# One attention and two-layer feed-forward kernel on one core: a different start-up (centroids, zeros, square root) and a new order of the planned work

## The chip, the cores and the metric

The kernel runs on one core of a Trainium2 chip. The metric is the device time of one execution, in microseconds (us). Three executions of the kernel before took 782.28, 782.38 and 784.30 us; their median, 782.38 us, is the time before.

The names of the engines are those of the profile: PE is TensorE, DVE is VectorE, ACT is ScalarE, POOL is GpSimd, SP is the engine whose queue issues the transfers. PEld is the loading of weights into PE, which overlaps with PE. A line such as L640 is line 640 of the kernel before.

## What is computed

Attention in which a query sees only the keys of its own cluster, for 2 x 8 heads of 768 rows and 64 columns, followed by two feed-forward stages:

```python
q_n, k_n, c_n = (each row divided by its norm + 1e-6)
q_assign = argmax(einsum('bhsd,hcd->bhsc', q_n, c_n), axis=-1)   # 16 clusters a head
k_assign = argmax(einsum('bhsd,hcd->bhsc', k_n, c_n), axis=-1)
scores = where(q_assign == k_assign, q @ k.T / 8, -1e9)
x = (softmax(scores) @ v)            # to 1536 tokens x 512
h = x @ w_in;  y = (h - tanh(h)) @ w_out
out = (sigmoid(y @ w_gate) * (y @ w_val)) @ w_out2
```

The assignment needs the norms of the centroids only (a query's own norm does not change its argmax), so the kernel normalises `centroids` and leaves `q` and `k` as they are.

## The kernel before

**The planner.** Nearly all work is written down as tasks: `add(engine, cost, priority, function, dependencies, buffers)`. The class `Planner` (from L271) then plays them through with the modelled costs and emits the functions in the order that comes out. The priority of task n is `ORDER[n] / 1000`, from a list of numbers that a search made (L39 on); among the tasks of an engine that could start within a window (`AHEAD`, from the parameters `AH_PE` to `AH_SP` at L27) the one with the lowest number goes first. Each engine then works through its own queue strictly in the order emitted, and waits on the chip for what an instruction needs.

**What is not planned.** What is written straight into the function, outside `add`, comes ahead of all planned work of its engine, and the planner's clock knows nothing of it. Before L613 that is: the filler's operand `busy` (L583), the identity matrices (L586 to L588), small constants on POOL (L589 to L601), and the zeros:

```python
for i in range(NS):                                   # L606, NS = 3 buffers "stk"
    if PRM["NAT"]:
        nc.vector.memset(tiles["stk", i].bitcast(F32)[0:96]...., 0.0)   # L608, 96 x 3072
    nc.gpsimd.memset(tiles["stk", i].bitcast(F32)[96:97, 3, :], 1.0)    # L609
```

**The start-up.** `rawq` and `rawk` (the first two heads, 2 x 192 KB each) and `rawv` are loaded by SP (L710, L908). Between the two loads SP issues that of the centroids, `cn` (L625). The centroids are normalised by three planned tasks: `cn_square` on ACT (L628 square with the row sum in `ss`, L629 square root, L630 one exponential that serves to load the table of the exponential again), `cn_scale` on DVE (L633 to L635), and a transpose on PE (L640); `cn_place` on DVE (L645) puts the result into `cb`. Meanwhile PE transposes `rawq` and `rawk` (L721, three at a time, two halves each, in the order q, k, q, k), ACT copies the results out as `xtq`, `xtk` (L725), and for the first two heads ACT and POOL write their high and low parts into `stk` (L737, L741). With `cb`, `xtq` and `xtk` PE makes the 24 scores of the clusters (L772); DVE finds the winners and makes them one-hot (L781 to L792); PE turns them (L863), ACT writes them into `stk` (L867). After that the heads' work proper begins: matmuls L936, L1003 and L1056, exponentials L1006 and L1059, low parts on POOL and DVE L1022 and L1070, products with `v` L1082 to L1084. The feed-forward part follows (L1369, L1732), for which the weights are loaded, cut and split meanwhile.

**The filler.** 110 planned tasks of two small matmuls on zeros (L652, operand `busy`) have the lowest priority of PE; the planner puts one wherever PE could start nothing else, until all 110 are used up. Their number (`N_BUSY`) is the same before and after, and the psum bank that they write is free for other work only after the last of them.

Of the kernel before, what the change touches and what calls it, by code (L numbers as in the profile page):

```python
# [27 lines left out]
    QUEUE=2.4, AH_PE=0.1147, AH_ACT=0.2895, AH_DVE=0.0311, AH_POOL=2.0837, AH_SP=1.2656, N_BUSY=110, NR=2,  # L28
    NRH=1, HX=['hx', 'hhxx'], WAR=0.8, LM=9, LV=9, ZP1=-12.307, ZP=1.419, FD=0.1631, FO=0.8005, LOQ=0, VHI=0,
# [399 lines left out]
def tile_cluster_attention_moe(  # L429
# [41 lines left out]
    def c_acts(n):  # L471
        return 0.10 + 0.00084 * n
# [73 lines left out]
    NS = 3  # L546
# [59 lines left out]
    for i in range(NS):  # L606
        if PRM["NAT"]:
            nc.vector.memset(tiles["stk", i].bitcast(F32)[0:96].rearrange("p a n -> p (a n)"), 0.0)  # L608
        nc.gpsimd.memset(tiles["stk", i].bitcast(F32)[96:97, 3, :], 1.0)  # L609
# [1326 lines left out]
```

## Time and profile before

| | before |
|---|---|
| median of three executions | 782.38 us |
| the profiled execution: its own time | 784.97 us |
| the profiled execution: span from first to last instruction | 782.8 us |
| PE busy | 770.6 us (98% of the span) |
| DVE, ACT, POOL busy | 73%, 58%, 72% |
| share of PE in the chain that ended last | 93% |

The page of a profile gives the busy time of each engine, the chain of work that ended last (followed back from the last instruction to what released it) and the costliest groups of instructions. The trace behind it can be asked for the busy time in chosen stretches, the waits of an engine with what ended them, and the instructions in order of time. A busy PE is not a useful PE: the filler counts as busy, and so does a matmul that runs at half clock.

### The profile page before, as it was taken

Reading aid. Unit: us, or ns where it says so; the run is one execution under the profiler, and the core shown is the slowest. Engines: PE = TensorE matmul, PEld = TensorE weight load, DVE = VectorE, ACT = ScalarE, POOL = GpSimd, SP = SyncE. Lnnn points to the kernel's source line nnn. Section 1 sums busy time; section 2 is a strip of 40 time slices with the busy share of each in tenths; the row PEclk is TensorE's granted clock in tenths of the full one; section 3 lists DMA queues with packets and bytes.
Section 4 is the critical chain, followed back from the end, with each engine's and each line's share of the span. In section 5 each row is a group of like instructions: output and inputs, shape, how many; then the busy total and the mean of one; then the engine's idle time right before and its main releaser. Section 6 shows DMA issues by size and latency. Waiting matters only on the chain.

```text
span 782.8 us, 15756 instructions
## 1 busy us (share of the span) xinstructions
PE 770.6 (98%) x5905; PEld 728.4 (93%) x5905; DVE 573.6 (73%) x1110; ACT 457.5 (58%) x883; POOL 567.1 (72%) x604
## 2 busy tenths in 40 slices
PE   7999999999999999999999999999999999999998
PEld 6988899898889999999999999999998989899997
DVE  6697878887986978877576878976465786765434
ACT  4588888889887644544554455765462635253250
POOL 6249777778979795787797699699593978665261
PEclk8999999999999999999999999999999999999999
DMA  4597755665642100422131323003220332310004
GB/s 103 133 182 157 165 128 137 145 154 133 152 129 81 59 1 0 135 69 68 54 95 41 108 68 107 14 29 107 68 82 27 98 119 69 93 63 20 1 1 161
DMA packets 75571, 69.57 MB, mean 89 GB/s; under 512 B 39252, under 2 KB 60072, under 8 KB 75496
## 3 DMA queue, kind: packets, MB, share of 16 engines
q1 hardware_dynamic: 75496, 68.58, 32.6%
q8 instruction: 46, 0.75, 0.4%
q14 instruction: 29, 0.24, 0.1%
HBM read 45.12 MB, written 3.15 MB: 62 GB/s over the span
## 4 chain that ended last, share of the span: by engine, by line
PE 93%; DVE 5%; ACT 1%; issue 1%; POOL 0%; DVEq 0%; ACTq 0%; POOLq 0%
PE over_left L1369 17%; PE over_left L1732 15%; PE sm L1732 10%; PE sm L1369 10%; PE over_right L1369 8%; PE over_right L1732 6%; PE bb L1056 3%; PE bc L1056 2%; PE ba L1056 2%; PE sm L1082 2%; PE sm L1083 2%; PE sm L1084 2%; PE sm L772 2%; PE ba L936 1%; DVE finr L940 1%; PE bc L936 1%
## 5 line engine op out<-in xcount | busy, mean ns | idle before, releaser
L1070 POOL TENSOR_TENSOR pt<-pf,pt 128x768 f16<-128x768 f32 x46 | 77.3, 1694 | 19.4 <-ACT pt L1059 9.5
L1070 POOL TENSOR_TENSOR ptt<-pf,ptt 128x768 f16<-128x768 f32 x29 | 49.8, 1723 | 13.4 <-ACT pf L1059 8.2
L1732 PE MATMUL over_left<-xh,stk 128*128 128x384 f32 x186 | 54.7, 335 | 0.0
L1369 PE MATMUL over_left<-stk,w 128*128 128x384 f32 x178 | 46.4, 337 | 0.0
L1082 PE MATMUL sm<-vs,pt 128*128 128x65 f16 x318 | 43.4, 194 | 0.2 <-DVE xl L1121 0.2
L1083 PE MATMUL sm<-vs,pt 128*128 128x64 f16 x318 | 43.2, 195 | 0.0
L1084 PE MATMUL sm<-vs,pt 128*128 128x65 f16 x318 | 42.9, 192 | 0.0
L1748 ACT ACTIVATE pf<-over_left 128x384 f32<-128x384 f32 x40 | 19.6, 489 | 33.0 <-PE over_left L1732 31.7
L940 DVE TENSOR_REDUCE finr<-ba 128x1 fp32r<-128x768 f32 x35 | 33.2, 948 | 5.6 <-PE ba L936 2.7
L1400 ACT ACTIVATE stk<-pf 128x384 fp32r<-128x384 f32 x43 | 22.3, 523 | 25.0 <-POOL pf L1803 6.9
L1402 POOL TENSOR_TENSOR oht<-pf,stk 128x384 fp32r<-128x384 f32 x23 | 23.4, 1018 | 16.5 <-ACT stk L1400 16.5
L1343 POOL TENSOR_TENSOR w<-ry,w 128x256 fp32r<-128x256 f32 x26 | 20.2, 788 | 20.5 <-ACT w L1341 15.9
L1082 PEld LDWEIGHTS <-pt 128*128 128x128 f16 x318 | 29.7, 96 | 5.4 <-issue 5.0
L940 DVE TENSOR_REDUCE finr<-bc 128x1 fp32r<-128x768 f32 x32 | 30.4, 949 | 5.9 <-PE bc L936 5.7
L1732 PEld LDWEIGHTS over_left<-xh,stk 128*128 128x128 f32 x186 | 34.3, 188 | 0.3
L1732 PE MATMUL over_left<-sum,stk 128*128 128x384 f32 x127 | 33.7, 338 | 0.0
L1056 PE MATMUL bb<-stk 112*128 112x384 f32 (+2 forms) x146 | 33.6, 353 | 0.0
L1756 ACT ACTIVATE pf<-pf 128x384 f32<-128x384 f32 x33 | 17.3, 523 | 27.7 <-DVE pf L1752 27.6
L1083 PE MATMUL sm<-vs,ptt 128*128 128x64 f16 x222 | 33.1, 195 | 0.0
L1402 POOL TENSOR_TENSOR stk<-pf,hlk 128x384 fp32r<-128x384 f32 x20 | 21.1, 1056 | 16.6 <-ACT hlk L1400 16.6
L1082 PE MATMUL sm<-vs,ptt 128*128 128x65 f16 x222 | 33.0, 193 | 0.0
L1732 PE MATMUL over_left<-xl,stk 128*128 128x384 f32 x98 | 32.8, 335 | 0.0
(617 smaller groups left out, 3135.2 us busy)
## 6 DMA issues: line engine op xcount, KB each, us to landing
vs<-in_moe_w_out_dram SPq DMA_DIRECT2D x48, 256.0 KB, 2.6
vs<-in_moe_w_in_dram SPq DMA_DIRECT2D x24, 256.0 KB, 2.6
vs<-in_moe_w_val_dram SPq DMA_DIRECT2D x24, 256.0 KB, 2.7
vs<-in_moe_w_gate_dram SPq DMA_DIRECT2D x24, 256.0 KB, 2.9
stk<-hlq SPq DMA_DIRECT2D x28, 192.0 KB, 2.7
stk<-hlk SPq DMA_DIRECT2D x14, 384.0 KB, 4.4
rawq<-in_q_dram SPq DMA_DIRECT2D x16, 192.0 KB, 3.3
rawk<-in_k_dram SPq DMA_DIRECT2D x16, 192.0 KB, 3.7
```

Of the source, the lines that this page charges most:

```text
L940: rd.append(use(mx, add(DVE, c_dve(S), z + t, lambda t=t, mx=mx: nc.vector.tensor_reduce(at(mh)[:, t:t + 1], at(mx)[:, :, 0:HALF], axis=AX ...
L1056: nc.tensor.matmul(o, at(sk)[0:n, l_, ts], at(sk)[0:n, m_, c], start=i == 0, stop=i == len(terms) - 1)
L1070: lambda nce=nc.vector if on_v else nc.gpsimd, pf=pf, pt=pt: nce.tensor_tensor(at(pt)[:, 1], at(pf), at(pt)[:, 0], op=ALU.subtract), [e0, ...
L1082: nc.tensor.matmul(oview()[:, t], ph, vv[:, 0:D + 1], start=(kt == 0), stop=False)
L1083: nc.tensor.matmul(oview()[:, t, 0:D], ph, vv[:, D + 1:2 * D + 1], start=False, stop=False)
L1084: nc.tensor.matmul(oview()[:, t], plo, vv[:, 0:D + 1], start=False, stop=(kt == T - 1))
L1343: e1 = add(POOL, c_pool(PIECE), z, lambda o=o, cut=cut: nc.gpsimd.tensor_tensor(at(w[1])[:, o], f32_of(cut), at(w[0])[:, o], op=ALU.subtra ...
L1369: nc.tensor.matmul(ps, a, b, start=(i == 0), stop=(i == n - 1))
L1400: a = add(ACT, c_acts(CH), z, lambda: nc.scalar.activation(hi(), src(), AF.Copy), deps, take)
L1402: nc.vector if on_v else nc.gpsimd).tensor_tensor(lo(), src(), hi(), op=ALU.subtract), [a], port=True)
L1732: nc.tensor.matmul(at(bank[to])[:, 0:CH], lh, rh, start=start and i == 0, stop=stop and i == 3 * KH - 1, skip_group_check=True)
L1748: t = use(bank[n], add(ACT, c_act(CH), rank[0], lambda: nc.scalar.activation(at(x), ps(n), AF.Copy), [dep], [x]))
```

## The change

Five things change. `ORDER` is replaced as a whole by another list, and the five `AH_` parameters with it (the table of `PRM` is otherwise the same). Of the zeros only those are left that the first two heads need: in `stk` 0 half of the columns of 64 rows on DVE, in `stk` 1 all columns of 64 rows on POOL, in `stk` 2 none; the row of ones (L609) is written for `stk` 2 and 0 only. The centroids are loaded by a DMA that ACT issues, ahead of its other work; the planned task `t_cl` stays on SP but does nothing. A dummy square root on a scalar `warm` follows on ACT at once. The square and its row sum move from ACT to two instructions of DVE that come ahead of all its planned work. And the planned cast L737 checks which `stk` buffer its head was given.

```diff
-    QUEUE=2.4, AH_PE=0.1147, AH_ACT=0.2895, AH_DVE=0.0311, AH_POOL=2.0837, AH_SP=1.2656, N_BUSY=110, NR=2,
+    QUEUE=2.4, AH_PE=0.1219, AH_ACT=0.29, AH_DVE=0.0344, AH_POOL=5.5247, AH_SP=2.0746, N_BUSY=110, NR=2, NRH=1,
...
-    for i in range(NS):
-        if PRM["NAT"]:
-            nc.vector.memset(tiles["stk", i].bitcast(F32)[0:96].rearrange("p a n -> p (a n)"), 0.0)
+    if PRM["NAT"]:
+        nc.vector.memset(tiles["stk", 0].bitcast(F32)[D:2 * D, 2:4].rearrange("p a n -> p (a n)"), 0.0)
+        nc.gpsimd.memset(tiles["stk", 1].bitcast(F32)[0:D].rearrange("p a n -> p (a n)"), 0.0)
+    for i in (2, 0) if PRM["NAT"] else range(NS):
         nc.gpsimd.memset(tiles["stk", i].bitcast(F32)[96:97, 3, :], 1.0)
...
     cn = left_p.tile([H * C, D], F32, name="cn")
+    warm = const.tile([1, 1], F32, name="warm")
+    nc.vector.memset(warm, 0.0)
     sq = left_p.tile([H * C, D], F32, name="sq")
     ss = left_p.tile([H * C, 1], F32, name="ss")
-    t_cl = add(SP, DMA_C, -199, lambda: dma(cn, centroids.rearrange("h c d -> (h c) d")), lat=0.2)
+    nc.scalar.dma_start(cn, centroids.rearrange("h c d -> (h c) d"))
+    nc.scalar.activation(warm, warm, AF.Sqrt)
+    nc.vector.tensor_tensor(sq, cn, cn, op=ALU.mult)
+    nc.vector.tensor_reduce(ss, sq, axis=AX.X, op=ALU.add)
+    t_cl = add(SP, DMA_C, -199, lambda: None, lat=0.2)
 
     def cn_square():
-        nc.scalar.activation(sq, cn, AF.Square, accum_out=ss)
         nc.scalar.activation(ss, ss, AF.Sqrt)
-        nc.scalar.activation(sq[:, 0:1], sq[:, 0:1], AF.Exp)
+        nc.scalar.activation(warm, warm, AF.Exp)
...
-                a = add(ACT, c_acts(S), zn, lambda xt=xt, sk=sk, rw=rw, x=x: nc.scalar.activation(
-                    at(sk)[rw, x], at(xt)[rw], AF.Copy), ev[nm] + own[hh][1:2], [sk] if len(own[hh]) == 1 else [])
+                def cast(xt=xt, sk=sk, rw=rw, x=x, hh=hh):
+                    assert sk.item == hh
+                    nc.scalar.activation(at(sk)[rw, x], at(xt)[rw], AF.Copy)
+
+                a = add(ACT, c_acts(S), zn, cast, ev[nm] + own[hh][1:2], [sk] if len(own[hh]) == 1 else [])
```

The planned costs are as before (`t_c1`, which holds `cn_square`, still counts as 3.0 us on ACT), and so are the number of tasks and what each depends on. The new list is some 3,500 numbers like the old one and cannot be read by eye.

## Rows read from the trace of the kernel before

**Rows 1.** Stretch, length, busy PE, PEld, DVE, ACT, POOL (xcount), clock, DMA share, GB/s.
```profile
0.00:12.99 12.99, 7.17 (x70) 6.28 (x71) 10.30 (x9) 8.93 (x15) 6.12 (x36) 0.97 0.52 129
12.99:19.63 6.64, 6.64 (x41) 6.58 (x42) 2.58 (x9) 0.34 (x1) 6.10 (x4) 0.54 0.24 51
40.00:200.00 160.00, 157.49 (x1922) 143.33 (x1923) 132.15 (x224) 140.20 (x208) 123.19 (x82) 1.00 0.67 149
200.00:760.00 560.00, 559.32 (x3537) 537.29 (x3536) 404.67 (x824) 295.18 (x641) 422.13 (x476) 1.00 0.22 68
```

**Rows 2.** PE and PEld of the filler L652 alone: one stretch, 0 to 200 us.
```profile
19.63:40.00 20.37, 10.60 (x150) 8.55 (x147) 1.00 0.59 136
sum 200.00, PE 17.52 PEld 15.09; mean PE 4.38 PEld 3.77
```

**Rows 3.** What PE waited for: total, times, longest, in us.
```profile
PE smr L640 <- DVE cn L635: 3.2, 1, 3.2
```

**Rows 4.** The chain that ended last, 0 to 48 us: start, duration, what.
```profile
2.16 2.62 DVE stk L608
...
8.57 2.62 DVE stk L608
...
11.45 1.50 DVE cn L635
...
13.41 1.28 PE sm L652 x12
...
32.09 0.80 PE sm L652 x14
...
34.86 0.04 DVE finr L940
```

**Rows 5.** PE in order of time: start, duration, what [idle before <-releaser].
```profile
4.95 0.77 PE L721 MATMUL ba<-ident,rawq 128*128 128x128 f32 x3 [0.57 <-POOL stk L609]
...
7.23 0.53 PE L721 MATMUL bb<-ident,rawk 128*128 128x128 f32 x3 [0.84 <-DMA rawk<-in_k_dram]
...
8.82 0.55 PE L721 MATMUL ba<-ident,rawq 128*128 128x128 f32 x3 [0.17 <-ACT xtq L725]
9.20 0.54 PE L721 MATMUL bb<-ident,rawk 128*128 128x128 f32 x3
12.99 0.42 PE L640 MATMUL smr<-ident,cn 128*64 128x128 f32 x1 [3.25 <-DVE cn L635]
```

**Rows 6.** The other engines in order of time, 2 to 23 us.
```profile
2.17 0.64 SPq L625 DMA_DIRECT2D cn<-in_centroids_dram  x1
...
5.00 0.26 ACT L628 ACTIVATE sq<-cn 128x64 f32<-128x64 f32 x1 [2.98 <-DMA cn<-in_centroids_dram]
...
6.89 1.28 ACT L630 ACT_TABLE_LOAD   x1
...
8.29 0.47 ACT L725 ACTIVATE xtq<-ba 128x384 f32<-128x384 f32 x1
...
21.14 0.35 DVE L792 TENSOR_TENSOR oh<-smr,mm 128x192 bf16<-128x192 f32 x1
...
22.09 0.84 PE L863 MATMUL smr<-ident,oh 128*16 128x128 bf16 x12
```

**Rows 7.** Columns as in rows 1: one microsecond after PE's wait.
```profile
13.00:14.00 1.00, 1.00 (x9) 0.94 (x10) 0.99 (x3) 0.33 (x1) 1.00 (x1) 0.50 1.19 266
```

**Rows 8.** L772 alone: 24 matmuls of pair 1, 24 of pair 0.
```profile
28.10:31.10 3.00, 2.87 (x24) 2.70 (x24) 1.00 0.93 211
14.70:19.65 4.95, 4.93 (x24) 4.76 (x24) 0.55 0.01 3
```

**Rows 9.** Transfers, and the zeros and ones of POOL.
```profile
2.50:6.50 4.00, 3.32 (x33) 2.89 (x31) 3.41 (x2) 1.48 (x3) 2.55 (x8) 1.00 0.91 207
...
L609 POOL MEMSET stk<- x3: 732/732/737, 2.8 to 4.1; 1x768 f32 x3
```

**Rows 10.** The costliest group of POOL, from the page.
```profile
L1070 POOL TENSOR_TENSOR pt<-pf,pt 128x768 f16<-128x768 f32 x46 | 77.3, 1694 | 19.4 <-ACT pt L1059 9.5
```

More of the change, by code (lines that the diff above doesn't have):

```diff
@@ L27 @@
 PRM = dict(
-    QUEUE=2.4, AH_PE=0.1147, AH_ACT=0.2895, AH_DVE=0.0311, AH_POOL=2.0837, AH_SP=1.2656, N_BUSY=110, NR=2,
-    NRH=1, HX=['hx', 'hhxx'], WAR=0.8, LM=9, LV=9, ZP1=-12.307, ZP=1.419, FD=0.1631, FO=0.8005, LOQ=0, VHI=0,
+    QUEUE=2.4, AH_PE=0.1219, AH_ACT=0.29, AH_DVE=0.0344, AH_POOL=5.5247, AH_SP=2.0746, N_BUSY=110, NR=2, NRH=1,
+    HX=['hx', 'hhxx'], WAR=0.8, LM=9, LV=9, ZP1=-12.307, ZP=1.419, FD=0.1631, FO=0.8005, LOQ=0, VHI=0,
     ZV0=-23.288, VR=40.471, ZSV=-53.844, ZRAW=10.895, ZT=1.445, ZH=70.02, ZHL=13.774, ZS=6.68, ZC=-1.658,
```

407 rows, old and new, of the table ORDER are left out of this document.

## The prediction

> **What bounds the kernel now.** First the busy time by stage [rows 1]: from 200 to 760 us PE is busy for 559.32 of 560 us at full clock, so PE itself is the bound there and an order can give back 0.7 us at most. From 40 to 200 us it is busy for 157.49 of 160. Before 12.99 us it is busy for only 7.17, and from 12.99 to 19.63 us it is always busy at a mean clock of 0.54. What is not useful PE time lies at the start. Busy is not useful there, though: the filler takes 17.5 us of PE, 10.60 of them between 19.63 and 40 us [rows 2].
>
> Next the waits of PE [rows 3]: by far the longest is 3.2 us, of the transpose L640 for the centroids. The chain that ended last says what made it late [rows 4]: three zeros of 2.62 us each on DVE, the last from 8.57 us, and only behind them `cn_scale`, which ends at 11.45 + 1.50. The zeros are not planned work, so the order of PE's queue does not allow for them. After 12.99 us the chain holds PE alone, in its own order, until DVE comes back into it at 34.86 us. So what PE is spared before 19.63 us moves everything behind it.
>
> PE in order of time [rows 5] gives the position of L640: the last transposes of `rawk` end at 9.20 + 0.54 = 9.74 us, nothing stands between, and PE then waits 3.25 us. After that wait the granted clock is 0.50 [rows 7], that is 1.2 GHz. The same 24 matmuls of the scores take 4.95 us there and 2.87 us at 28 us with the clock at 1.00, 2.4 GHz [rows 8].
>
> **The change part by part.** *The zeros.* Three of 2.62 us with gaps, 2.16 to 11.19 us, become half of one on DVE: 1536 elements in place of 3072, 1.31 us, so DVE is free at about 3.5. POOL gets 3072 elements: a row of 768 takes it 0.732 us [rows 9], so 4 x 0.732 = 2.93 us, and one row less. POOL is busy for only 6.12 of the first 12.99 us [rows 1], so its idle time takes this in, and it costs nothing unless something on PE waits for POOL's rows (a rival below).
>
> *The centroids.* In the trace they are issued at 2.17 and used at 5.00 us, 2.83 later, behind `rawq` in one queue [rows 6]. ACT can issue at about 0.75, so by the same 2.83 they land at 3.6. SP is spared 0.64 us of issue, so that `rawk` could land up to 0.64 earlier; but the transfer engines are 0.91 busy from 2.5 to 6.5 us [rows 9], and the same bytes have to pass. I take 0 of [0, 0.64]. Issuing on ACT costs ACT about the 0.64 that it costs SP, in a time when ACT waits 2.98 us for the centroids anyway [rows 6].
>
> *Squares and tables.* Two ops of DVE in the place of one of ACT: the nearest ACT op takes 0.26 us [rows 6], the scores' ops on DVE on three times the columns 0.35; at most 0.35 each, so the sums stand at 3.6 + 0.7 = 4.3. Behind the two on DVE wait `cn_scale` and the first maximum of `rawv`, nothing earlier. The table of the root is loaded while the centroids travel. The root (no longer than the square, 0.26 us) and the load of the other table (1.28) [rows 6] end at about 5.9 in place of 8.2, and ACT can copy `xtq` 2.3 us earlier than 8.29. That removes the 0.17 us for which PE waits for it [rows 5]. It brings no more: `rawk` holds PE up to 7.23, and between the end of its first transposes at 7.76 and 8.82 PE idles for 0.17 us only, the rest being filler of its own queue [rows 5].
>
> *L640.* `cn_scale` can run at 4.6 to 6 us, 3 us or more before PE reaches L640. So the 3.25 us go whole: **3.25**. What is late next is PE's own queue.
>
> *The clock.* Without that gap I expect the clock to stay at 1.00, as it does in the mean until then (0.97 over the whole stretch with the gap in it [rows 1]) in spite of waits of 0.84 and 0.57 us [rows 5]. Then the 24 score matmuls take 2.87 in place of 4.95 (2.08 less), and the twelve fillers before them 12/14 of 0.80 = 0.69 in place of 1.28 (0.59 less) [rows 4, 8]: **2.67**. The bounds are 0 (the clock falls all the same) and 2.67 + 0.3 for the two small transposes among them. DVE then has to follow: its one-hot of `q` ends at 21.49 and PE wants it at 22.09 [rows 6], 0.6 of slack, of which the faster matmuls behind `q`'s scores use 0.3. So no new wait here.
>
> The Trainium skill has a rule on this, in the page "TensorE: Matmul & The Clock Gate", Part 1: the clock follows how busy the engine has lately been, and the point at which it changes differs from run to run of one kernel. By it the 2.67 could also come out as 0; I make that a rival.
>
> *The new order.* The number of fillers is fixed, so a better order cannot drop them; it can only replace idle time. Reachable are 2.51 us between 40 and 200 and 0.68 after that [rows 1], 3.2 in all; a worse order could add as much idle as there is, 2.5. Between -2.5 and +3.2 no row favours either end much; I take the middle, **0.5** rounded up, and keep both ends.
>
> *The empty task* on SP and the check in the cast cost nothing: SP is spared an issue, and the check is made when the program is written.
>
> **The sum.** The profiled execution took 784.97 us: 784.97 - 3.25 - 2.67 - 0.5 = 778.55. It stands 2.59 above the median, 782.38; so the median should become 778.55 - 2.59 = **776.0**.
>
> **The rivals.** (a) *The clock falls all the same.* PE's start stays patchy: it is busy for 7.17 of 12.99 us [rows 1], and the waits for `rawq` and `rawk` remain. Then only 3.25 + 0.5 go: 778.6. Against it: a mean of 0.97 up to 12.99 us [rows 1] leaves room for a fall only near the end of that stretch, that is in the long gap. Chance 0.12.
>
> (b) *POOL's new zero holds up PE's first transposes.* The first of them at 4.95 is put down to the rows of ones on POOL, L609 [rows 5], which end in the trace just before it. If it truly waits for them and not for `rawq`, it starts when POOL is through, 2.8 + 2.93 + 2 x 0.73 = 7.2 in place of 4.95. From there to 9.74 PE works 4.79 - 0.84 - 0.17 = 3.78 us [rows 5], so L640 starts at 11.0 and 2.0 of the 3.25 are left: 777.2. Against it: the transposes read nothing that L609 writes, and `rawq` lands about then. Chance 0.08.
>
> (c) *The centroids land late,* with `rawk` at 7.2 [rows 5] in place of 3.6. Squares, root and table then end at 7.2 + 0.7 + 0.26 + 1.28 = 9.4, `xtq` comes 1.1 later than now, and with it L640: 777.1. The page "DMA: Bandwidth & Descriptors" of the Trainium skill (Queues, rings and completion order) says that an engine takes turns between the queues that have work, which speaks against it; no row here shows it, all transfers being in one queue. Chance 0.05.
>
> (d) *The gain is given back between 35 and 60 us.* The chain leaves PE at 34.86 for DVE [rows 4]. If DVE and ACT there are the true bound and the new order starts their part no earlier, the 5.9 us turn into waits of PE: about 782. Against it: DVE's work there starts from PE's results, which come earlier too. Chance 0.07.
>
> (e) *Slower: POOL falls behind in the heads.* The new window of POOL, 5.5 us in place of 2.1, lets the planner put off a low part that is due. PE's products with `v` need all six of a head, each 1.69 us on POOL [rows 10]. Half of one late in each of 16 heads is 0.85 x 16 = 13.6: 776.0 + 13.6 = 789.6. It decides from 6.4 / 16 = 0.4 us per head on; below that some gain is left. Against it: PE's waits in this stage sum to 2.5 us, and POOL is busy for only 123 of 160 us there [rows 1]. Chance 0.07.
>
> That the change does not do what it says can be excluded for the zeros and the centroids: they stand outside the plan and come first on their engines whatever the order.
>
> **How the numbers follow.** The forecast, full clock and all of the 3.25, has 0.61. Its own range goes from 772 (the order gives 3.2, `rawk` lands 0.64 earlier, 0.3 more from the clock) to 779 (the order takes 2.5). To (a) at 778.6 with some loss by the order the range reaches 780.5; (b) and (c) lie inside. Left out are (d), (e) and a part of (a). About 0.3% (2.35 us) is what a measurement of this kernel can tell from no change; below 780.0 lie the forecast, (b), (c) and most of (a): faster 0.84. Within it (d) and the rest of (a): same 0.09. Slower is (e): 0.07.
>
> **What would show it.** In the profile after: DVE free of zeros by 4 us; the squares at about 3.6; ACT's second table load ended by 6; L640 near 9.7 with no wait; L772 from about 11 in under 3 us at clock 1.00; the filler still 220 matmuls; the span about 776.5. It is wrong if L640 still waits, if the clock is 0.50 at 12 to 18 us, if PE's first transposes wait for POOL, or if PE's idle time between 40 and 200 us rises from 2.5 by several us.

## The result and the profile after

Five executions of the changed kernel took 776.50 to 778.23 us, median 777.96, against 782.38 before (five executions, 780.84 to 785.21). The recorded ratio is 0.9917, 95% interval 0.9896 to 0.9937; the interval lies below 1, so the kernel is faster, by about 0.8%. The two medians alone make 0.9944, outside that interval; the record does not say why the two differ. The repeats e5 and e11, with 29 and 11 executions of before beside them, gave 0.9930 and 0.9923. The forecast was 776.0 in a range of 772.0 to 780.5.

The profiled execution took 776.54 us, its span is 774.8. The first two lines of its page:

```profile
span 774.8 us, 15780 instructions
PE 767.1 (99%) x5905; PEld 725.4 (94%) x5905; DVE 568.4 (73%) x1111; ACT 457.6 (59%) x881; POOL 569.9 (74%) x604
```

Busy time by stage, columns as in [rows 1]:

```profile
0.00:12.99 12.99, 10.48 (x111) 9.82 (x112) 6.03 (x18) 7.94 (x13) 8.44 (x36) 1.00 0.58 138
12.99:19.63 6.64, 6.64 (x100) 5.85 (x98) 5.74 (x12) 4.20 (x7) 5.93 (x4) 1.00 0.15 33
40.00:200.00 160.00, 158.80 (x2001) 144.07 (x2000) 134.12 (x229) 140.31 (x208) 128.40 (x86) 1.00 0.67 148
200.00:752.00 552.00, 551.52 (x3427) 531.33 (x3423) 395.76 (x812) 289.49 (x631) 416.08 (x471) 1.00 0.21 67
```

PE is busy for 10.48 of the first 12.99 us in place of 7.17, and between 13 and 19.6 us it gets through 100 matmuls in place of 41, at clock 1.00 in place of 0.54. Between 40 and 200 us its idle time has fallen from 2.51 to 1.20. What it still waits for before 13 us is its first operand and the transfers; the wait of L640 (L647 after) is gone:

```profile
PE sm L659 <- DVE busy L584: 1.0, 1, 1.0
PE ba L728 <- DMA rawq<-in_q_dram: 0.7, 1, 0.7
PE bb L728 <- DMA rawk<-in_k_dram: 0.7, 1, 0.7
```

The start in order of time. The lines moved with the change: L608 and L609 are zeros, L629 the load of the centroids, L631 and L632 squares and sum, L637 the other table, L642 the end of `cn_scale`, L728 the transposes, L732 the copies of `xtq` and `xtk`, L647 the transpose of the centroids, L782 the scores, L1013 the heads' first matmuls.

```profile
0.74 0.38 ACTq L629 DMA_DIRECT2D cn<-in_centroids_dram  x1
...
2.32 1.34 DVE L608 MEMSET stk<- 64x1536 f32 x1 [0.36 <-issue]
...
2.65 2.65 POOL L609 MEMSET stk<- 64x3072 f32 x1
...
3.69 0.22 DVE L631 TENSOR_TENSOR sq<-cn 128x64 f32<-128x64 f32 x1
...
4.42 1.28 ACT L637 ACT_TABLE_LOAD   x1
...
4.83 0.53 DVE L642 TENSOR_SCALAR cn<-cn,ss 128x64 f32<-128x64 f32 x1
...
5.06 0.52 PE L728 MATMUL ba<-ident,rawq 128*128 128x128 f32 x3 [0.74 <-DMA rawq<-in_q_dram]
...
6.95 0.52 PE L728 MATMUL bb<-ident,rawk 128*128 128x128 f32 x3 [0.70 <-DMA rawk<-in_k_dram]
...
7.50 0.49 ACT L732 ACTIVATE xtk<-bb 128x384 f32<-128x384 f32 x1 [1.58 <-PE bb L728]
...
9.14 0.27 PE L647 MATMUL smr<-ident,cn 128*64 128x128 f32 x1
...
10.12 0.88 PE L782 MATMUL sm<-cb,xtk 128*128 128x96 f32 x6
...
19.81 1.31 PE L1013 MATMUL ba<-stk 80*128 80x384 f32 x6
```

L647 starts at 9.14 us without a wait, where L640 started at 12.99 after 3.25 us of it [rows 5]. The scores by themselves, columns as in [rows 8]:

```profile
10.05:13.05 3.00, 2.89 (x24) 2.75 (x24) 1.00 0.88 199
```

**Where the span of 8.0 us went.** Three marks cut each profile into start, heads and rest: the first matmul of a head (L1003, 26.18 us before; L1013, 19.81 after), the last product with `v` (252.7 before; 244.7 after), and the end.

```profile
L1082 PE MATMUL sm<-vs,pt x318: 190/192/208, 68.2 to 252.7; 128*128 128x65 f16 x159
```

```profile
L1092 PE MATMUL sm<-vs,pt x318: 190/192/206, 61.2 to 244.7; 128*128 128x65 f16 x159
```

(The view of one line: name, count, shortest/median/longest ns, first and last start.) Taking each mark from such rows:

| profiled execution | start | heads | rest | span |
|---|---|---|---|---|
| before | 26.2 | 226.5 | 530.1 | 782.8 |
| after | 19.8 | 224.9 | 530.1 | 774.8 |
| e1, new start, old order | 19.2 | 226.5 | 530.8 | 776.5 |
| e2, old start, new order | 25.4 | 225.2 | 531.3 | 781.9 |
| e3, zeros only | 21.5 | 226.6 | 530.0 | 778.1 |
| e4, gap filled | 24.1 | 227.8 | 530.1 | 782.0 |
| e5, after again | 20.7 | 225.1 | 530.0 | 775.8 |
| e6, before again | 26.6 | 226.6 | 530.2 | 783.4 |
| e7, centroids only | 27.1 | 226.6 | 530.8 | 784.5 |
| e8, without 75 fillers | 19.8 | 226.7 | 529.9 | 776.4 |
| e9, xtq first | 19.3 | 225.2 | 530.6 | 775.1 |
| e10, xtq first and six fillers | 19.5 | 225.0 | 530.0 | 774.5 |
| e11, after, control | 21.2 | 225.5 | 530.0 | 776.7 |
| e12, before, third | 25.9 | 227.1 | 531.1 | 784.1 |

From before to after the start is 6.4 us shorter, the heads 1.6, the rest the same to 0.1. Over all profiles the rest varies by 1.4 us, so less than that in a single pair proves little.

### The profile page after: what moved, and what is told of

Same layout as the page of the kernel before. It is cut to its first block, busy times and chain, and to the rows that moved or that the text cites. A ratio compares the mean times of both kernels' runs of the same rounds, so it can differ in the third digit from the quotient of the medians.

```text
span 774.8 us, 15780 instructions
## 1 busy us (share of the span) xinstructions
PE 767.1 (99%) x5905; PEld 725.4 (94%) x5905; DVE 568.4 (73%) x1111; ACT 457.6 (59%) x881; POOL 569.9 (74%) x604
## 4 chain that ended last, share of the span: by engine, by line
PE 93%; DVE 3%; ACT 1%; issue 1%; DMA 1%; SPq 0%; DVEq 0%; ACTq 0%
PE over_left L1379 23%; PE over_left L1742 21%; PE over_right L1379 7%; PE over_right L1742 6%; PE sm L1379 6%; PE sm L1742 4%; PE bc L1066 3%; PE sm L782 2%; PE ba L1066 2%; PE bb L1066 2%; PE sm L1092 2%; PE sm L1093 2%; PE sm L1094 2%; PE ba L946 2%; PE bb L946 1%; PE sm L659 1%
## 5 line engine op out<-in xcount | busy, mean ns | idle before, releaser
L1742 PE MATMUL over_left<-xh,stk 128*128 128x384 f32 x228 | 70.8, 336 | 0.0
L1762 DVE TENSOR_TENSOR pf<-over_left,pf 128x384 f32<-128x384 f32 x62 | 34.3, 554 | 40.2 <-ACT pf L1758 24.5
L1410 ACT ACTIVATE hlk<-pf 128x384 fp32r<-128x384 f32 x44 | 22.9, 523 | 35.7 <-POOL pf L1772 13.7
L1379 PE MATMUL over_left<-hlk,w 128*128 128x384 f32 x154 | 43.4, 336 | 0.0
L1742 PE MATMUL over_left<-xh,ry 128*128 128x384 f32 x124 | 39.9, 336 | 0.0
L1412 POOL TENSOR_TENSOR hlq<-pf,hlk 128x384 fp32r<-128x384 f32 x25 | 25.8, 1032 | 16.1 <-ACT hlk L1410 16.1
L1758 ACT ACTIVATE pf<-over_left 128x384 f32<-128x384 f32 x44 | 21.4, 488 | 27.1 <-PE over_left L1742 27.1
L1379 PE MATMUL over_left<-w,stk 128*128 128x512 f32 (+1 forms) x108 | 37.0, 391 | 0.0
L1497 DVE TENSOR_TENSOR ptt<-over_left,ptt 128x384 f32<-128x384 f32 x58 | 31.5, 550 | 6.8 <-PE over_left L1379 6.8
L1066 PE MATMUL bc<-stk 112*128 112x384 f32 (+2 forms) x150 | 34.7, 354 | 0.2 <-DVE finr L950 0.2
L1353 POOL TENSOR_TENSOR w<-vs,w 128x256 fp32r<-128x256 f32 x25 | 19.8, 803 | 20.1 <-ACT w L1351 20.1
```

The source lines that it names most:

```text
L1066: nc.tensor.matmul(o, at(sk)[0:n, l_, ts], at(sk)[0:n, m_, c], start=i == 0, stop=i == len(terms) - 1)
L1379: nc.tensor.matmul(ps, a, b, start=(i == 0), stop=(i == n - 1))
L1412: nc.vector if on_v else nc.gpsimd).tensor_tensor(lo(), src(), hi(), op=ALU.subtract), [a], port=True)
L1497: u = add(DVE, c_dve(CH), z, lambda a=a, src=src: nc.vector.tensor_tensor(a(), src(), a(), op=ALU.add), [t] + prev)
L1742: nc.tensor.matmul(at(bank[to])[:, 0:CH], lh, rh, start=start and i == 0, stop=stop and i == 3 * KH - 1, skip_group_check=True)
L1762: return use(x, use(bank[n], add(DVE, c_dve(CH), rank[0], lambda: nc.vector.tensor_tensor(at(x), ps(n), at(x), op=ALU.add), deps)))
```

## The experiments

**e1, the new start with the old order.** The changed kernel with `ORDER` and the `AH_` parameters of before (in short):

```diff
-ORDER = (the new list);  AH_PE=0.1219, AH_ACT=0.29, AH_DVE=0.0344, AH_POOL=5.5247, AH_SP=2.0746
+ORDER = (the old list);  AH_PE=0.1147, AH_ACT=0.2895, AH_DVE=0.0311, AH_POOL=2.0837, AH_SP=1.2656
```

> The start of the changed kernel (zeros, centroids, squares, root's table) with the old list of priorities and the old AH_ parameters. Theory (the start brings the gain): the transpose of the centroids comes at 9.1 to 9.8 us with no wait, the clock is 1.00 from 12 to 19 us, the 24 score matmuls take under 3 us, and the first matmuls of the heads come some 6 us earlier than the 26.2 us of before; the time is 5 to 6 us under that of before, about 776.5 to 777.5. Rival (the order brings it): the heads start no earlier than 24 us or the time lies within 1.5 us of before.

Measured: 0.9948 (0.9928 to 0.9968), median 779.26 us. The centroids' transpose starts at 8.77 us with no wait, the scores take 2.89 us, and the heads start at 19.18, 7.0 us earlier than before.

```profile
8.77 0.27 PE L646 MATMUL smr<-ident,cn 128*64 128x128 f32 x1
```

The start alone makes the kernel faster; the median is higher than expected, as that of before on this chip was too (784.57).

**e2, the old start with the new order.** The reverse exchange in the kernel before.

> The start of the kernel before (three zeros of 96 x 3072 on VectorE, centroids through SP, square on ScalarE) with the new list and the new AH_ parameters. Theory: TensorE again waits about 3 us for the centroids and runs the scores at half clock; the time is 0.5 to 2 us under before (781.9 to 780.4). Rival (the order brings the gain): 778 or less. Second rival (the new order needs the new start): slower than before.

Measured: 0.9984 (0.9964 to 1.0003), median 782.55. PE waits 3.29 us again and the clock falls to 0.50, here from 13.1 to 16.5 us.

```profile
13.35 0.42 PE L641 MATMUL smr<-ident,cn 128*64 128x128 f32 x1 [3.29 <-DVE cn L636]
```

The heads take 225.2 us, as with the new order in the changed kernel (224.9 to 225.5), and not 226.5 as with the old one. So the order is worth about 1.4 us in the heads; the interval of the time just includes none, and in this profile the rest is 1.2 us longer than in that of before. The two factors make 0.9948 x 0.9984 = 0.993, and the whole change measures 0.9917 and, in e5 and e11, 0.9930 and 0.9923.

**e3, the zeros alone.** The kernel before with (cut at the dots)

```diff
-    for i in range(NS):
-        if PRM["NAT"]:
-            nc.vector.memset(tiles["stk", i]...[0:96]..., 0.0)
+    if PRM["NAT"]:
+        nc.vector.memset(tiles["stk", 0]...[D:2 * D, 2:4]..., 0.0)
+        nc.gpsimd.memset(tiles["stk", 1]...[0:D]..., 0.0)
+    for i in (2, 0) if PRM["NAT"] else range(NS):
```

> The kernel before with only the zeros changed; centroids still through SP, square on ScalarE, old order. Theory (the zeros alone hold the centroids up): the centroids are scaled by 8 us, their transpose follows those of rawk at about 9.7 us with no wait, clock 1.00, time 5.5 to 6 us under before, equal to e1 within 0.5 us. Rival (the centroids' path through SP and ScalarE's two table loads is late too): the transpose waits 1 us or more, and e1 is faster by as much.

Measured: 0.9949 (0.9931 to 0.9967), the same as e1. So the zeros held the centroids up, and once they are gone the centroids' new path gives nothing that can be measured. The profile holds a surprise. `rawk` came late in this execution (a wait of 1.39 us), and behind that wait the clock was at half rate (columns as in rows 1):

```profile
8.00:9.00 1.00, 1.00 (x12) 0.98 (x10) 0.58 (x1) 0.99 (x4) 0.00 (x0) 0.50 0.00 0
9.00:10.00 1.00, 1.00 (x11) 1.00 (x10) 0.38 (x1) 0.17 (x1) 0.00 (x0) 0.50 0.00 0
10.00:11.00 1.00, 1.00 (x6) 0.97 (x5) 0.00 (x0) 0.39 (x1) 0.00 (x0) 0.50 0.00 0
```

There is no gap of 3.25 us here at all: a fall of the clock does not need that gap.

**e4, the gap filled with matmuls.** The kernel before with 29 more pairs of filler ahead of L640:

```diff
+    def cn_turn():
+        for _ in range(29):
+            keep_busy()
+        nc.tensor.transpose(at(z_sm)[0:D, 0:H * C], cn, ident)
```

> The kernel before with 58 more filler matmuls (128 x 128, bf16, zeros) in TensorE's queue just ahead of the transpose of the centroids, where TensorE waits 3.25 us; nothing else. The transpose comes at about 13 us as before. Theory (the gap is what lowers the clock): the clock stays at 1.00 from 12 to 19 us, the 24 score matmuls take 2.9 us in place of 4.95, and the time is about 2.7 us under before. Rival (the clock falls there all the same): 0.50 after 12 us, 4.9 us for the scores, time as before.

Measured: 0.9999 (0.9982 to 1.0016). The clock does stay up, and the scores take 2.89 us:

```profile
14.60:17.55 2.95, 2.89 (x24) 2.75 (x24) 1.00 0.16 35
```

The heads start at 24.08 us, 2.1 earlier than in the profile of before. Yet the time did not move: over twelve executions (783.14 to 785.17 us) the gain expected is not there. Part of what ate it can be seen in the profile. The transpose starts at 13.34 us in place of 12.99, and the heads take 227.8 us in place of 226.5; in them PE waits twice, 0.6 us in all, for a transfer into `stk` (`stk<-mt`), which no other profile with the old order shows. The rest was not found. So the edit did more than keep the clock up, and it does not show that the half clock costs nothing. The price of 2.67 us in my sum is seen in the records of the start, and not in the time of this experiment.

**e5, the changed kernel again.**

> The changed kernel once more, on one chip with e6 to e8 and with many runs of before. Theory (start about 4 to 5 us, order 1 to 2): ratio 0.990 to 0.994 to before, granted clock 1.00 from 9 us on in the profile. If the start of e1 were all: 0.995.

Measured: 0.9930 (0.9904 to 0.9957), median 777.93. Start 20.7 us, heads 225.1. The start is 0.9 us longer than in the first profile: `rawq` came 0.5 us later (first transposes at 5.52), and PE ran at half rate until about 9 us. The record shows that in the matmuls, not in its clock: two groups of twelve fillers and the clock over them.

```profile
6.18 1.49 PE L659 MATMUL sm<-busy 128*128 128x128 bf16 x12
...
10.14 0.83 PE L659 MATMUL sm<-busy 128*128 128x128 bf16 x12
...
6.00:8.00 2.00, 2.00 (x17) 1.94 (x16) 0.08 (x1) 0.00 (x0) 1.04 (x5) 1.00 0.55 179
```

**e6 and e12, the kernel before again.**

> The kernel before against itself, with a second profile of it: what a comparison of two equal kernels gives, and whether the clock falls at the same place. Theory (the point at which the clock falls differs from run to run, and the 2.67 us of the prediction came from one execution that lost much): ratio 1.000 within 0.002; the half clock lies at another time or lasts for another length than 12.3 to 19.1 us in this profile. Rival (the fall belongs to the gap of 3.25 us): again 0.50 from about 12.5 to 19 us.

> A third profile of the kernel before. Theory (its executions differ by how long the clock is at half rate behind the gap of 3.25 us): an execution of 781 to 782 us has the 24 scores in clearly less than 4.9 us and its heads start at 24 us or earlier; one of 784 us or more has them in 4.9 to 5.5 us and starts at 26 us or later. Rival (the spread has another source, later on): the start is as in the first two profiles whatever the time.

Measured: e6 against itself 1.0013 (0.9993 to 1.0033); its twelve executions lie between 781.43 and 786.03. Its profile (785.52 us) has the half clock from 13.7 to 20.3 us, the 24 scores in 5.4 us, the start at 26.6. e12 (786.19 us; 781.34 in the execution beside it) has it from 11.7 to 18.5, the scores in 4.6 and the start at 25.9; in the first profile of before it lasts from 12.3 to 19.1. So the place of the fall differs from execution to execution, as expected; its length, 6.6 to 6.8 us in these three, does not. For its time e12 should have had the scores in 4.9 us or more and the start at 26 or later. It has neither: what makes it 1.3 us longer than the first profile lies behind the start (heads 227.1, rest 531.1). So the fall of the clock is not the only source of the spread.

All three profiles of before are of 784.97 us or more; none is of the short kind. But the record gives for every execution its granted clock, averaged over the span. Of the 76 executions of before in e1 to e11 (64 beside the experiments, 12 in e6) 17 read 1.00, and all of these took 781.2 to 782.9 us, median 781.5. Of the 59 that read 0.993 to 0.998, 49 took 783.4 us or more and 10 took 781.2 to 782.2. Beside e5 to e8 the two kinds are plain: 14 executions of 781.2 to 782.2 us, half of them at 1.00, and 15 of 783.4 to 788.0, none at 1.00. So no execution that kept its clock was long, and a lower clock went with a longer time in most, not in all. The changed kernel reads 1.00 in 16 of 17 executions (this result, e5, e11), with a median of 777.9. At 1.00 on both sides the change is thus worth 3.6 us; e1 alone comes to 2.5 (779.1) and e2 to 1.1 (780.5, three executions). And e4, at 1.00 in nine of twelve, is with 784.0 us some 2.5 slower than before at 1.00: its edit cost about what the clock gave back. These are comparisons of executions; no run sets the clock by itself, and a reading of 1.00 does not exclude half rate in the first 10 us (e5).

**e7, the centroids' part alone.** The kernel before with the load from ACT, the dummy root and the squares on DVE, and the three zeros left where they are (the lines of the diff from `cn` to `cn_square`).

> The kernel before with only the centroids' part changed: issued by ScalarE, squares on VectorE ahead of its planned work, root's table first; the three zeros of 96 x 3072 stay on VectorE ahead of the squares; old order. Theory (the zeros on VectorE decide): the squares now come behind the zeros at 11.2 us, ScalarE's root and the load of the other table behind them end at about 13.3, so that ScalarE copies xtq 5 us later than before and the transpose of the centroids comes at about 14.9 in place of 12.99: 2 to 4 us slower than before. Rival (the centroids' path brings a gain of its own): as fast as before or faster.

Measured: 1.0040 (1.0024 to 1.0056), slower: 0.4%, 3.1 us. The squares stand behind the zeros, ACT's root and table behind the squares, and `xtq` behind those:

```profile
8.58 2.62 DVE L608 MEMSET stk<- 96x3072 f32 x1 [0.59 <-issue]
11.12 0.22 DVE L629 TENSOR_TENSOR sq<-cn 128x64 f32<-128x64 f32 x1
...
11.85 1.28 ACT L635 ACT_TABLE_LOAD   x1
...
12.25 0.25 DVE L640 TENSOR_SCALAR cn<-cn,ss 128x64 f32<-128x64 f32 x1
...
13.77 0.90 PE L726 MATMUL ba<-ident,rawq 128*128 128x128 f32 x3 [5.53 <-ACT xtq L730]
...
15.11 0.42 PE L645 MATMUL smr<-ident,cn 128*64 128x128 f32 x1
```

PE now waits 5.53 us for ACT, and the transpose comes at 15.11, 0.2 later than worked out. The part that is worth nothing behind the shortened zeros costs 3 us without them.

**e8, without the last 75 fillers.** The changed kernel with

```diff
-        fill.append(add(PE, 0.111, 1e6, keep_busy, fill[-1:], tail=0.055))
+        fill.append(add(PE, 0.111, 1e6, keep_busy if i < 35 else (lambda: keep_busy(0)), fill[-1:], tail=0.055))
```

> The changed kernel without the last 75 of the 110 fillers (150 of 220 matmuls, all behind the first scores); nothing else. Theory (behind the start VectorE, ScalarE and GpSimd set the pace, and the filler only fills TensorE's waiting): the heads' first matmuls come less than 1 us earlier, TensorE idles for about 8 us more before 40 us, and the time is the same within 1 us, or worse if the clock falls in the gaps. Rival (the filler stands in the way, being in TensorE's own order): up to 3 us faster than the changed kernel.

Measured: 0.9990 (0.9968 to 1.0012), median 782.98 in executions from 778.22 to 784.48: slower than the changed kernel by 0.6%. That is more than the 1 us of the theory; its reserve, that the clock falls in the gaps, is what came. The heads start at 19.77, as in the changed kernel, so the filler is not in the way. But PE idles, and its clock falls in the first heads (columns as in rows 1):

```profile
25.00:30.00 5.00, 2.89 (x8) 1.79 (x9) 4.93 (x12) 0.45 (x1) 3.54 (x3) 0.67 1.05 211
30.00:35.00 5.00, 5.00 (x21) 4.39 (x21) 3.79 (x6) 2.42 (x5) 0.00 (x0) 0.50 0.69 131
```

That profile is of the shortest execution of the twelve, and the others lost more clock: the four of 778.2 to 779.9 us read 0.990 to 0.993 over their span, the eight of 782.6 to 784.5 read 0.986 to 0.989.

**e9 to e11, two moves in the new start.** In the changed kernel ACT idles 1.58 us with `xtq`'s transposes done and copies `xtk` first, presumably because the order still counts with 3.0 us for `cn_square`. e9 moves two things in the list that the planner emits; e10 adds six fillers ahead of the first transposes; e11 is the changed kernel beside them. The diff is cut, and its comments are added here.

```diff
+        i = seq.index(trs[1])
+        seq[i:i] = moved                            # 16 fillers, ahead of rawk's first transposes
+        evs = [t for t in seq if t.eng == "ACT" and name(t) == "evac"]
+        seq.remove(evs[1])
+        seq.insert(seq.index(evs[0]), evs[1])       # xtq ahead of xtk
         for t in seq:
+            if t is trs[0]:                         # e10 only
+                for _ in range(3):
+                    trs_busy()
             t.fn()
```

> The changed kernel with two moves in the order it emits: ScalarE copies the first half of xtq ahead of that of xtk (in the changed kernel it sits idle from 5.9 to 7.5 us with xtq's transposes done), and the 16 fillers between the first transposes of rawk and the second of rawq go ahead of the former, where TensorE waits for rawk. Theory (behind the start everything hangs on when the scores begin, and all of it moves together): the scores begin 0.5 to 0.8 us earlier than in the control of this call, the heads' first matmuls too, and the time falls by the same 0.5 to 0.8. Rival (GpSimd or the transfers set the heads' start): the scores come earlier, the heads and the end do not.

> As e9, with six more fillers just ahead of the very first transposes, where TensorE waits 0.7 to 1.1 us for rawq. Theory (the early waits leave the clock at half rate up to 9 us in some executions): the matmuls of 5 to 9 us run at full rate more often, the executions lie closer together, and the median is up to 0.5 us under e9. Rival (the six only push the transposes back): e9 or up to 0.5 us slower.

> The changed kernel as control for e9 and e10 on the same chip: 776.5 to 778.5 us.

Measured against before: e9 0.9919 (0.9896 to 0.9942), median 777.30; e10 0.9912 (0.9889 to 0.9934), median 776.70; e11 0.9923 (0.9899 to 0.9948), median 777.90. In the profiles the scores begin at 9.59 us (e9), 9.82 (e10) and 11.53 (e11, where PE was at half rate until about 10.5), against 10.12 in the first profile after, and the heads at 19.3, 19.5 and 21.2. The six fillers of e10 did not bring the full rate at 5 us: its first transposes take 0.87 us, against 0.52 in e9. The medians stand in the expected order, e10 lowest, with executions of 776.31 to 778.27; the intervals overlap almost wholly. A gain of 0.6 to 1.2 us is likely, not shown.

## Why the prediction was right, point by point

*The zeros on DVE hold the centroids up, the 3.25 us go.* Right, and shown by e3: with the zeros alone changed the ratio is that of the whole new start. But the delay by the zeros themselves is only about 2 of the 3.25: the other 1.2 is the last step of `cn_scale`, which takes 1.49 us beside POOL and 0.25 with POOL idle (see the last section). The prediction read its end, 11.45 + 1.50, and did not ask why it took so long. DVE was through with its one zero at 3.66 us (3.5 worked out), POOL's took 2.65 (2.93).

*The centroids' path.* They were used at 3.69 us (3.6 worked out), DVE's two ops took 0.22 each (at most 0.35), the issue took 0.38 of ACT's queue (0.64), ACT was through with root, table and dummy at 5.92 (5.9). That ACT could then copy `xtq` 2.3 us earlier did not come about: the new order puts `xtk` first, and `xtq` is copied at 7.89 in place of 8.29. It was priced at the 0.17 us of PE's wait, so the sum did not suffer.

*`rawk` lands no earlier: 0 of [0, 0.64].* Too low: 6.95 in place of 7.23 us in the two first profiles, 0.3. That is half of why L647 starts at 9.14 and not at 9.7; it also starts 0.16 before the modelled end of the transposes ahead of it (8.81 + 0.49), and 9.7 was such an end. The landing varies by more than that between executions (7.56 in e3).

*The clock, 2.67.* In the profile pair it is right to 0.1: the scores take 2.89 us at clock 1.00, and the start as a whole shortened by 6.4 where 5.9 was forecast. As a term of the median it was counted whole, and it belongs only to those executions of before that lose their clock: at 1.00 on both sides the change is worth 3.6 us, where the forecast without this term is 3.75. The rule of the page "TensorE: Matmul & The Clock Gate" of the Trainium skill (Part 1) that the point of change differs from run to run (the page says it of the rise) agrees with three profiles of one kernel: the half rate covers 12.3 to 19.1 us in the first, 13.7 to 20.3 in e6, 11.7 to 18.5 in e12. And rival (a) was put too simply: in e3 the half rate lies earlier, behind the wait for `rawk`, and in e5 and e11 the matmuls run at half rate from the start to about 9 and 10.5 us. In e11, where `rawq` came as in the first profile (5.09 us against 5.06), that costs 1.4 us of the start.

*The order, 0.5 of [-2.5, 3.2].* Undersized: the heads are 1.3 to 1.6 us shorter with it in the profiles after, e2 and e5, and 1.0 in e11. In the first pair about 1.3 of that is idle time between 40 and 200 us. The bound held.

*The sum.* The step that failed is the conversion: "it stands 2.59 above the median, so the median should become" the sum less 2.59. That took the distance of one execution from the median for a property of the kernel. Most likely it also took the same loss off twice: the 2.59 is about the 2.67 already taken off for the clock, and the executions of before at 1.00 have a median of 781.5, below 782.38. Without the 2.59 the sum stands at 778.55, 0.6 above what was measured. The clocks of the executions in the median of before are not on record, so this is not shown. The profiled execution of before was one of the long ones (784.97 of 780.84 to 785.21), that of after one of the short (776.54 of 776.50 to 778.23). Profile against profile the forecast was 6.4 us and 8.4 came; median against median 6.4 and 4.4. That the median came within 2 us of the forecast is in part luck: the terms were 2.0 too small between the profiles, the conversion was 4.0 off (2.59 taken off, where the profile after stands 1.4 under its median), and the first cancels half of the second. By the ratio, 0.9917 of 782.38 is 6.5 us less. The executions of before spread over 4 to 7.5 us and those of after over under 2, so a single one of before was worth little as a base.

*The rivals.* (b) is out: PE's first transposes start at 5.06, while POOL's zero runs to 5.30, so they do not wait for it; e1's profile names that zero before the same transposes, at 5.33, but they followed it there only in time. (c) is out: the centroids were there by 3.69; that the queues take turns, as the page "DMA: Bandwidth & Descriptors" of the Trainium skill (Queues, rings and completion order) states, agrees with a load that was in use 2.95 us after its issue with `rawq` still on its way until 5.06. (d) is out: the lead at the heads' start is there at the end. (e) is out: PE's idle time in the heads fell.

## What to carry to other kernels

Work written outside a planned order comes ahead of everything that is planned on its engine, so it has to be priced by hand: three memsets that no plan knew of held up one small chain, and every later matmul with it. Where a chain crosses engines, moving a step to another engine helps or hurts by what is queued there ahead of it: the same lines cost 3 us behind the long zeros and nothing behind the short one. A forecast of a median needs the spread of the executions, not the distance of one profile from their middle; and a loss that only some executions have counts in it only by their share.

## What the runs showed that was not expected

The granted clock in the record stood at 1.00 between 6 and 8 us in e5 while twelve fillers took 1.49 us, and 0.83 for the same twelve at 10 us: at the start the spacing of the matmuls tells the rate, the record does not. The same holds before: its first transposes took 0.77 us [rows 5], against 0.52 after, under a recorded 1.00, so the mean of 0.97 on which the prediction leaned says little of the first 6 us.

The filler that looks like waste holds the clock up for the heads: without 150 of its small matmuls the clock fell there and the median went from 777.9 to 783.0 us (e8).

The centroids' last step before L640 was itself held up. The scaling of 128 x 64 values, planned at 0.5 us together with the two steps before it, took 1.49 us by itself in the kernel before:

```profile
11.08 1.80 POOL L741 TENSOR_TENSOR stk<-xtq,stk 64x768 fp32r<-64x768 f32 x1 [5.91 <-ACT stk L737]
11.45 1.49 DVE L635 TENSOR_SCALAR cn<-cn,ss 128x64 f32<-128x64 f32 x1
```

It ends 0.06 us after POOL's first low part, and in e2, e4, e6 and e12, where that low part begins at 11.02 to 11.44 us, it ends 0.05 after it too (1.42 to 1.84 us). With POOL idle it takes 0.25 us (e7 at 12.25, e3). In the changed kernel it takes 0.53 and ends 0.06 after POOL's zero, at 5.36. So the zeros made the centroids late, and by that put their scaling beside POOL's low part, for another 1.2 us. It is also why the transpose comes 0.35 later in e4, whose low part begins at 11.42. That POOL holds it up is read from these ends; no run moves the low part alone.

Two ops of DVE that scale `v` ran longer than before, because they now fall beside POOL's low parts (L751, from 14.45 to 18.35 us):

```profile
15.17 1.50 DVE L926 SCALAR_TENSOR_TENSOR vs<-rawv,sv,vs 128x384 f16<-128x384 f32 x1
16.59 0.34 DVE L802 TENSOR_TENSOR oh<-sm,mm 128x192 bf16<-128x192 f32 x1
16.86 1.90 DVE L926 SCALAR_TENSOR_TENSOR vs<-rawv,sv,vs 128x384 f16<-128x384 f32 x1
```

In the kernel before, with POOL idle, the same op took 0.61 us, as it does in the changed kernel at 30.62:

```profile
30.62 0.60 DVE L926 SCALAR_TENSOR_TENSOR vs<-rawv,sv,vs 128x384 f16<-128x384 f32 x1
```

The op between the two, which takes one operand from psum, kept its 0.34. The page "SBUF — State Buffer" of the Trainium skill (Who interferes with whom) says that an op of VectorE with two inputs in SBUF contends with a GpSimd op that reads SBUF; these rows agree. What it costs in time here was not tested.
